# A new loading order for K, V and the later weights, with a new order of all instructions, in a fused long-convolution and feed-forward kernel

## The chip, the cores and the metric

The kernel runs on 1 core of one Trainium2 chip. The metric is the device time of one execution in microseconds; three runs of the kernel before gave 193.63, 193.73 and 193.83.

## The reference

```python
def reference(A_q, A_k, A_v, A_shift_k, A_ssm_k, A_ssm_D, B_x, B_w_gate, B_w_up, B_w_down):
    def _A_ref(q, k, v, shift_k, ssm_k, ssm_D):
        ...                                  # k_shift: k shifted by 0..3 tokens, times 4 taps, summed
        kv = k_shift * v
        ...                                  # y: causal convolution of kv with ssm_k over 2048 tokens (FFT)
        y = y + kv * ssm_D[None, None, :]
        return q * y

    def _B_ref(x, w_gate, w_up, w_down):
        g = jnp.einsum("bsd,df->bsf", x, w_gate)
        u = jnp.einsum("bsd,df->bsf", x, w_up)
        h = _gelu(g) * u
        return jnp.einsum("bsf,fd->bsd", h, w_down)

    x = A_q
    xn = _layernorm(x, axis=-1)
    s = _A_ref(xn, A_k, A_v, A_shift_k, A_ssm_k, A_ssm_D)
    g = _silu(_B_ref(xn, B_w_gate, B_w_up, B_w_down))
    return x + s * g
```

All arrays are bfloat16; q, k and v are 1 x 2048 x 512, the filter ssm_k is 512 x 2048, the gate and up weights 512 x 1792, the down weight 1792 x 512.

## The kernel before

The 2048 tokens stand as 16 tiles of 128, in four quarters (q = 0 to 3) of four tiles.

**Feed-forward.** Each quarter of x is normalized (statistics on VectorE at L832 and L833, a power on GpSimd at L841, the scaled product XN at L850 on ScalarE or L851 on VectorE) and transposed into xnT. Quarters 0 and 1 are transposed on TensorE (L872, four transposes a tile, tasks psxn) and copied out by ScalarE or VectorE; quarters 2 and 3 by a transposing DMA. For quarters 1 to 3 ScalarE's XN needs a bias that GpSimd makes in two steps (NB, L845 and L846). Then 14 units a quarter: a gate product (psg) and an up product (psu), each four matmuls of 512 columns (L626), GELU on ScalarE (GE, L1175) and the product of both on VectorE (HT, L1178). Units 0 and 1 of quarter 0 are made in two halves of 256 columns (L1166, L1168). The down products (psd) follow in pieces of 4, 5 and 5 matmuls, then tanh on ScalarE (L1202) and G on VectorE (L1204).

**Convolution.** It is a two-step transform of 2 x 2048 points. The filter h is transposed on TensorE (L896, psh, two groups of four for each of four pieces), copied to HTr, gets ssm_D added (fold, L910), and goes through step 1 (L938, ps1H0 to ps1H7) and two copies by ScalarE with a sum by VectorE (AH, L947) into DRAM (ZH). K is shifted on VectorE in four pieces: one product with a tap (KAC, L987), three more products (KTM, L991), three sums (KAC, L993) and the product with V's piece (V, L995, in what follows the "V product"). Each step works on 128 x 2048 elements. V's piece then goes through step 1 (L930, ps1K0 to ps1K7, two for each V piece), is copied by ScalarE and stored to DRAM (ZK). Step 2 of both (L1010; psf for the filter, psk for K) reads them back; the spectra are multiplied on VectorE, transformed back (psi, then psy at L1248), and joined with the feed-forward part.

**Banks.** PSUM's eight banks serve all of it. Feed-forward products take one bank each (at most four at once), a step of the transforms takes four, in two pairs of neighbours.

**Order.** All of it is written down as 780 tasks. `SEQ` is a written list of the task numbers; a number with "b" runs on the second engine that the task allows (VectorE in place of ScalarE for a copy out of PSUM, ScalarE in place of VectorE for a normalization). `Sched.run` goes through the list and gives every engine its own tasks in that order, and every buffer its place: it takes the one that is free first by its own plan. `ORDER` is the order in which the loads are numbered, `LAND` the time in ns at which the plan takes each load to have landed. All loads go through SyncE's queue in the order of `SEQ`, so do the stores of K's step 1 (ZK), the loads of step 2 and the three transposing DMAs that make matrices of the inverse transforms (L1021; each waits for the one before it). The stores of the filter's step 1 (ZH) and of the spectra go through ScalarE's queue. Engines wait for each other by semaphores alone, so a task whose input is late holds up all that stands behind it on its engine.

Of the kernel before, what the change touches and what calls it, by code (L numbers as in the profile page):

```python
# [22 lines left out]
LN_EPS = 1e-5  # L23
TURN = 8192
N_WARM = 18
ORDER = "x00 h0 x01 w0 D0 h1 w1 x1 h2 h3 s0 k0 w2 k1 k2 w3 d0 d1 k3 v2 v3 v0 v1 x2 x3"
SEQ = (
# [22 lines left out]
)  # L50
NF_BANKS = 4
ISSUE = 470.0
LAND = {"h2": 15700, "h3": 17000, "sk": 19100, "kh1": 20400, "kh113": 20600, "kz": 10800, "k0": 21900, "wg2": 23400, "wu2": 25100, "k1": 26400, "k2": 27700, "wg3": 29100, "wu3": 30600, "wd0": 32700, "wd1": 34900, "k3": 36100, "v2": 37400, "v3": 38700, "v0": 39900, "v1": 41200, "x0_0": 4400, "h0": 5900, "x0_1": 7000, "D": 4000, "wg0": 7950, "wu0": 8800, "h1": 10100, "wg1": 11600, "wu1": 13100, "x1": 14400}
W_XT, W_SW, W_BK, W_BH, W_ZI, W_BI, W_ZK, W_MI, W_G1 = 765000, 735000, 667000, 688000, 274000, 714000, 690000, 329000, 150000
NC_PAIRS = 4
SMALL = 1.15 * 262144
# [347 lines left out]
def build_kernel(nc, A_q, A_k, A_v, A_shift_k, A_ssm_k, A_ssm_D, B_w_gate, B_w_up, B_w_down, out):  # L404
    with ExitStack() as es0:
# [102 lines left out]
        def dsem(name):  # L508
            return DSem(nc.alloc_semaphore(name), name)
# [88 lines left out]
        def dma(eng, out_ap, in_ap, sem, r, w):  # L598
            trk.dma(eng, lambda e: e.dma_start(out=out_ap, in_=in_ap), sem, r=r, w=w)  # L599
# [3 lines left out]
        def load(name, out_ap, in_ap, w_res, w_buf, nbytes, ring="SP", r=(), rb=()):  # L603
            sem = dsem("d_" + name)
            last_load[0] = S.add([("loads", ISSUE)], lambda e: dma(ring, out_ap, in_ap, sem, r, w_res), r=rb, w=w_buf, nbytes=nbytes, land=float(LAND[name]))

# [212 lines left out]

        for what in ORDER.split():  # L820
            if what[0] == "x" and len(what) == 3:
# [513 lines left out]
```

## Time and profile before

| What | us |
|---|---|
| median of three runs (lowest, highest) | 193.73 (193.63, 193.83) |
| the profiled execution's own time | 193.45 |
| its span, from the first to the last instruction | 191.7 |
| TensorE busy | 185.6 (97%) |
| VectorE busy | 170.0 (89%) |
| ScalarE busy | 135.9 (71%) |
| GpSimd busy | 14.6 (8%) |
| read from HBM, written to it | 27.39 MB, 14.68 MB |

The profile is of one execution. A row of a timeline gives the start and the duration in us, the engine (PE is TensorE, PEld its weight loads, DVE VectorE, ACT ScalarE, POOL GpSimd, SP SyncE), the line, the operation, output and inputs, how many instructions are merged, and in brackets how long the engine stood idle before them and what ended that. A row of waits gives the total in us, the number of times and the longest. Matmuls are pipelined: the next starts before the last one's recorded end. The granted clock of TensorE is at full speed in the whole span.

### The profile page before, as it was taken

To read this page: it belongs to the slowest core of one execution; us is meant where nothing else is said; L and a number is where in the kernel's file an instruction comes from. 1 tells how busy PE (TensorE), PEld (TensorE's weight loads), DVE (VectorE), ACT (ScalarE), POOL (GpSimd) and SP (SyncE) were. 2 spreads that over 40 slices of the span, in tenths; PEclk is the share of its full clock that TensorE was granted. 3 is DMA by queue.
4 is the path that set the end of the run, shared out by engine and by line. 5 is a ranking of instruction groups with operands and counts; after the bars stand their busy time and mean duration, and the time that the engine had idled before them with its cause. 6 is when DMAs were issued, how large, how long until landed. Compare 5 with 4: busy or idle time off the path is not lost.

```text
span 191.7 us, 3540 instructions
## 1 busy us (share of the span) xinstructions
PE 185.6 (97%) x1392; PEld 79.3 (41%) x1392; DVE 170.0 (89%) x248; ACT 135.9 (71%) x184; POOL 14.6 (8%) x31
## 2 busy tenths in 40 slices
PE   7999999999989999999999999999999999999993
PEld 2676443434333333334343434334434444443442
DVE  6889999995999999999698999999999967389865
ACT  3399997978757678889598978778689553244841
POOL 5310560000000000021200000000000000000000
PEclk9999999999999999999999999999999999999999
DMA  5999999999567498358999898995203064966173
GB/s 180 325 384 337 350 370 373 405 345 350 192 209 218 165 297 298 150 199 301 321 253 266 301 364 295 300 349 213 113 0 113 0 219 156 362 251 211 41 299 109
DMA packets 36422, 47.84 MB, mean 250 GB/s; under 512 B 7347, under 2 KB 26039, under 8 KB 36406
## 3 DMA queue, kind: packets, MB, share of 16 engines
q1 hardware_dynamic: 29878, 39.23, 62.4%
q10 hardware_dynamic: 6528, 8.39, 12.5%
q8 instruction: 11, 0.18, 0.4%
q14 instruction: 5, 0.04, 0.1%
HBM read 27.39 MB, written 14.68 MB: 220 GB/s over the span
## 4 chain that ended last, share of the span: by engine, by line
PE 60%; DVE 14%; SPq 13%; DMA 8%; issue 2%; ACT 1%; POOL 0%
PE psall L626 52%; SPq L599 13%; DMA V<-in_A_v_dram 6%; PE psall L1010 5%; DVE KTM L991 3%; DVE KAC L993 2%; PE psall L1248 2%; DMA X<-in_A_q_dram 2%; DVE V L995 2%; DVE stats L832 1%; DVE HT L1178 1%; DVE KAC L987 1%; PE psall L930 1%; DVE G L1204 1%; ACT AST L617 1%
## 5 line engine op out<-in xcount | busy, mean ns | idle before, releaser
L626 PE MATMUL psall<-xnT,Wu 128*128 128x512 bf16 (+1 forms) x232 | 55.1, 373 | 0.7 <-DVE G L1204 0.7
L626 PE MATMUL psall<-xnT,Wg 128*128 128x512 bf16 (+1 forms) x232 | 55.2, 372 | 0.3 <-ACT X L617 0.2
L626 PE MATMUL psall<-Wd,HT 128*128 128x512 bf16 (+2 forms) x238 | 53.1, 367 | 0.0
L1175 ACT ACTIVATE GE<-psall 128x512 bf16<-128x512 f32 x54 | 31.5, 600 | 17.0 <-PE psall L626 11.3
L1178 DVE TENSOR_TENSOR HT<-psall,GE 128x512 bf16<-128x512 f32 x54 | 36.1, 685 | 4.9 <-PE psall L626 4.3
L626 PEld LDWEIGHTS psall<-xnT,Wg 128*128 128x128 bf16 x232 | 21.3, 98 | 28.1 <-issue 1.9
L626 PEld LDWEIGHTS psall<-xnT,Wu 128*128 128x128 bf16 x232 | 21.1, 98 | 28.1 <-issue 3.0
L626 PEld LDWEIGHTS psall<-Wd,HT 128*128 128x128 bf16 x238 | 21.7, 98 | 26.6 <-issue 4.0
L617 ACT ACTIVATE BO<-psall 128x1024 bf16<-128x1024 f32 x18 | 18.0, 1024 | 11.5 <-PE psall L1248 8.3
L1113 DVE TENSOR_TENSOR HSW<-KB,HSW 128x2048 bf16<-128x2048 bf16 x16 | 19.2, 1219 | 0.0
L617 ACT ACTIVATE HSW<-psall 128x1024 bf16<-128x1024 f32 x16 | 15.8, 1032 | 1.5 <-PE psall L1010 1.5
L617 ACT ACTIVATE KB<-psall 128x1024 bf16<-128x1024 f32 x13 | 12.9, 1029 | 3.7 <-PE psall L1010 3.7
L991 DVE TENSOR_TENSOR KTM<-KK,SKB 128x2048 bf16<-128x2048 bf16 x12 | 14.6, 1221 | 0.1
L993 DVE TENSOR_TENSOR KAC<-KAC,KTM 128x2048 bf16<-128x2048 bf16 x12 | 14.7, 1221 | 0.0
L841 POOL TENSOR_TENSOR mv<-mv,NHALF 128x1 f32<-128x1 f32 (+1 forms) x7 | 6.8, 979 | 68.0 <-DVE mv L840 68.0
L832 DVE BATCH_NORM_STATS2 stats<-X 128x6 f32<-128x512 bf16 x16 | 10.5, 679 | 0.4 <-DMA X<-in_A_q_dram 0.4
L617 ACT ACTIVATE AST<-psall 128x1024 bf16<-128x1024 f32 x10 | 10.2, 1023 | 0.9 <-PE psall L930 0.8
L1204 DVE SCALAR_TENSOR_TENSOR G<-G,psall 128x512 bf16<-128x512 bf16 x12 | 7.9, 683 | 2.1 <-ACT G L1202 2.1
L1113 DVE TENSOR_TENSOR KB<-KB,HSW 128x2048 bf16<-128x2048 bf16 x8 | 9.6, 1220 | 0.1
L1136 DVE TENSOR_TENSOR HSW<-HSW 128x2048 bf16<-128x2048 bf16 x8 | 9.5, 1218 | 0.0
L1202 ACT ACTIVATE G<-psall 128x512 bf16<-128x512 f32 x12 | 7.1, 595 | 3.2 <-PE psall L626 3.0
L617 ACT ACTIVATE XN<-psall 128x1024 bf16<-128x1024 f32 x8 | 8.1, 1027 | 1.6 <-PE psall L938 1.4
(84 smaller groups left out, 164.1 us busy)
## 6 DMA issues: line engine op xcount, KB each, us to landing
BH<-ZH SPq DMA_DIRECT2D x8, 512.0 KB, 5.4
HSW<-HSW SPq DMA_DIRECT2D x16, 256.0 KB, 4.2
BK<-ZK SPq DMA_DIRECT2D x8, 512.0 KB, 6.4
ZI<-BO ACTq DMA_DIRECT2D x16, 256.0 KB, 3.2
BI<-ZI SPq DMA_DIRECT2D x8, 512.0 KB, 4.5
ZK<-AST SPq DMA_DIRECT2D x5, 512.0 KB, 3.8
Hn<-in_A_ssm_k_dram SPq DMA_DIRECT2D x4, 512.0 KB, 7.4
KK<-in_A_k_dram SPq DMA_DIRECT2D x4, 512.0 KB, 12.6
```

What stands on the lines that cost most here:

```text
L599: trk.dma(eng, lambda e: e.dma_start(out=out_ap, in_=in_ap), sem, r=r, w=w)
L617: return h.activation(o, i, ACTF.Copy, scale=scale)
L626: return h.matmul(o, lhsT=l, rhs=r, start=st, stop=sp)
L832: t_stats[t] = op([("DVE", 670.0)], lambda e, h, t=t: h.bn_stats(stats[:, t, :], X[:, t, :]), r=[bX[q][t % 4]], w=[bst[t]], rr=[R_X[t]], w ...
L991: op([("DVE", dur)], lambda e, h, j=j, m=m: h.tensor_tensor(KTM[:, m.slot, :, :], kk(j), sk(j), ALU.mult), r=need + [bSKB[j], a], w=[m], r ...
L993: op([("DVE", dur)], lambda e, h, m=m: h.tensor_tensor(KAC[:, a.slot, :, :], KAC[:, a.slot, :, :], KTM[:, m.slot, :, :], ALU.add), r=[m], ...
L1010: trk.op("PE", lambda h: h.matmul(ps(s, i)[b, :], lhsT=wt(col)[a, :], rhs=data(col)[a, :], start=n < 16, stop=n >= len(todo) - 16, tile_po ...
L1113: return hd.tensor_tensor(pair(KB, *(2 * DM * z for z in slots())) if to else x, k, x, ALU.mult)
L1136: return hd.tensor_tensor(x, x, y, ALU.add)
L1175: op([("ACT", act(512))], lambda e, h: h.activation(GE[:, g.slot, :], bank(pg), ACTF.Gelu_apprx_tanh), r=[pg], w=[g], rr=lambda: R_bank(pg ...
L1178: op([("DVE", dve(512, 1))], lambda e, h: h.tensor_tensor(HT[:, q % 2, m, :], bank(pu), GE[:, g.slot, :], ALU.mult), r=[pu, g], w=[bHT[q][m]],
L1204: op([("DVE", dve(512, 1))], lambda e, h, g=g, pc=pc: h.scalar_tensor_tensor(out=g, in0=g, scalar=1.0, in1=pc(), op0=ALU.add, op1=ALU.mult ...
```

## The change

Only the three tables at the head of the kernel change; no instruction is added or taken away. `ORDER` loads the pieces of K and V and the later weights in turn. `LAND` gets new times for the later loads. `SEQ` is a new list in all of its length, found with the plan's transfer times varied over four sets, and 24 tasks, all copies out of PSUM or normalizations, change between ScalarE and VectorE.

```diff
-ORDER = "x00 h0 x01 w0 D0 h1 w1 x1 h2 h3 s0 k0 w2 k1 k2 w3 d0 d1 k3 v2 v3 v0 v1 x2 x3"
+ORDER = "x00 h0 x01 w0 D0 h1 w1 x1 h2 h3 s0 k0 w2 k1 v0 w3 k2 v1 d0 d1 k3 v2 v3 x2 x3"
 SEQ = (
-    "16 17 18 0 19 2 7 8 9 4 20 21 22 23 10 5 3 11 24 67 6 1 68 76 25 26 65 66 73 27 77 78 87 91 74 75 86 90 28 69 70 29 71 30 31 49 48 79 72 32 82 "
...
+    "16 17 18 19 0 20 21 22 23 24 2 25 7 1 26 3 4 27 10 11 8 67 68 76 28 29 30 31 32 6 49 9 12 65 66 73 33 5 34 35 77 78 87 91 74 75 69 70 79 71 72 "
...
 )
-LAND = {... "k0": 21900, "wg2": 23400, "wu2": 25100, "k1": 26400, "k2": 27700, "wg3": 29100, "wu3": 30600, "wd0": 32700, "wd1": 34900, "k3": 36100, "v2": 37400, "v3": 38700, "v0": 39900, "v1": 41200, ...}
+LAND = {... "k0": 22000, "wg2": 24450, "wu2": 26000, "k1": 27350, "v0": 28700, "wg3": 30250, "wu3": 31800, "k2": 33150, "v1": 34500, "wd0": 36750, "wd1": 39000, "k3": 40350, "v2": 41700, "v3": 43050}
```

In `ORDER` x00 and x01 are the halves of quarter 0 of x, h the filter's pieces, w a gate and an up piece (two units each for w0 and w1 and four for w2 and w3), D the skip weights, s the taps, d the halves of the down weight.

Read by engine, with the tasks' names in place of their numbers, these stretches of the list are spoken of below.

TensorE, start, before and after:

```
before: warm-up psxn0_1 psxn0_0 psh0_1 psh0_0 psg0_1(half) psu0_1(half) psg0_0(half) psu0_0(half) psxn0_2 psxn0_3 psh1_1 psh1_0 ...
after:  warm-up psh0_1 psxn0_1 psh0_0 psxn0_0 psg0_0(half) psg0_1(half) psu0_0(half) psxn0_2 psh1_0 psxn0_3 psu0_1(half) psh1_1 psg0_3
        psg0_5 psu0_1(half) psu0_3 psg0_0(half) psu0_5 psh2_0 psg0_1(half) psh3_0 psh2_1 psh3_1 ps1H2 ...
```

VectorE after, from the copy of psh3_0 on (HTr: copies of filter transposes; AH: sums behind filter step 1; kac, ktm: KAC and KTM of K's pieces 0 to 3; KV: the V products):

```
HTr3_0 HT0_1(half) st7 mv1_3 mv1_2 fold HT0_0(half) mv1_0 mv1_1 var1 HTr3_1 AH2 kac0 HT0_4 ktm0 AH3 HT0_2 kac0 AH1 ktm0 HT0_7 kac0 kac1
HT0_8 HT0_9 ktm0 AH7 HT0_10 kac0 HT0_6 ktm1 HT0_13 kac1 AH6 HT0_12 ktm1 HT0_11 AH5 KV0 ... KV1 ... KV2 kac3 HT1_7 ktm3 HT1_1 kac3 HT1_4
ktm3 kac3 KV3 HT1_3 G G ...
```

GpSimd after the taps' load: `SKB3 SKB2 SKB0 power(q1) NB SKB1 NB` (before: four SKB, then power, NB, NB). ScalarE after, in the same stretch: `AH3 AH3 XN4 AH1 AH1 store ZH3 GE0_7 GE0_9 XN6 XN7 store ZH2 GE0_8` (before: `AH3 AH3 GE0_6 AH1 GE0_8 GE0_9 stores XN6 XN5 XN7 GE0_7`).

TensorE around the last V products: before `... psg1_0 psg1_4 psg1_6 ps1K5 psd0_1 psu1_4 psg1_11 ps1K7 psu1_6 psu1_11 ps1K6`, after `... psu1_4 ps1K5 psd0_1 psg1_0 psu1_3 psg1_11 psd0_1 ps1K7 psg1_5 psu1_0 ps1K6 psu1_11 psu1_5 psg1_6`.

SyncE behind the loads: before `G1 MI0 MI1 x3 ZK1 ZK2 ZK0 bh0 ZK3 x2`, after `ZK1 MI0 G1 ZK2 ZK0 x2 x3 ZK3 MI1 bh0` (G1, MI0 and MI1 are the transposing DMAs, bh loads of the filter's step 2).

More of the change, by code (lines that the diff above doesn't have):

```diff
@@ L52 @@
 ISSUE = 470.0
-LAND = {"h2": 15700, "h3": 17000, "sk": 19100, "kh1": 20400, "kh113": 20600, "kz": 10800, "k0": 21900, "wg2": 23400, "wu2": 25100, "k1": 26400, "k2": 27700, "wg3": 29100, "wu3": 30600, "wd0": 32700, "wd1": 34900, "k3": 36100, "v2": 37400, "v3": 38700, "v0": 39900, "v1": 41200, "x0_0": 4400, "h0": 5900, "x0_1": 7000, "D": 4000, "wg0": 7950, "wu0": 8800, "h1": 10100, "wg1": 11600, "wu1": 13100, "x1": 14400}
+LAND = {"x0_0": 4400, "h0": 5900, "x0_1": 7000, "D": 4000, "wg0": 7950, "wu0": 8800, "h1": 10100, "wg1": 11600, "wu1": 13100, "x1": 14400, "h2": 15700, "h3": 17000, "sk": 19100, "kh1": 20400, "kh113": 20600, "kz": 10800, "k0": 22000, "wg2": 24450, "wu2": 26000, "k1": 27350, "v0": 28700, "wg3": 30250, "wu3": 31800, "k2": 33150, "v1": 34500, "wd0": 36750, "wd1": 39000, "k3": 40350, "v2": 41700, "v3": 43050}
 W_XT, W_SW, W_BK, W_BH, W_ZI, W_BI, W_ZK, W_MI, W_G1 = 765000, 735000, 667000, 688000, 274000, 714000, 690000, 329000, 150000
```

42 rows, old and new, of the table SEQ are left out of this document.

## The prediction

> **What bounds the kernel now.** I read the page first, then the chain of waits, then the waits of TensorE and VectorE, then the timelines of the first 30 us and of 70 to 80 us.
>
> ```profile
> span 191.7 us, 3540 instructions
> PE 185.6 (97%) x1392; PEld 79.3 (41%) x1392; DVE 170.0 (89%) x248; ACT 135.9 (71%) x184; POOL 14.6 (8%) x31
> ```
>
> TensorE is busy for 185.6 of 191.7 us. A new order of the same instructions can only give back time in which TensorE stands still, or add some. The waits of TensorE are these (us in total, times, longest):
>
> ```profile
> PE psall L626 <- DVE AST L680: 1.2, 1, 1.2
> PE psall L626 <- DVE G L1204: 0.7, 1, 0.7
> PE psall L930 <- DVE V L995: 0.4, 1, 0.4
> PE psall L930 <- ACT G L1202: 0.3, 1, 0.3
> PE psall L626 <- ACT X L617: 0.2, 1, 0.2
> ```
>
> The first is the start. The other four make 1.6 us; they fall in the stage where K is shifted on VectorE and its transform (L930) runs between the feed-forward products. The chain of waits says what that stage hangs on:
>
> ```profile
> 35.01 12.22 DMA V<-in_A_v_dram
> ...
> 68.30 0.63 PE psall L930 x4
> 68.93 4.65 PE psall L626 x21
> ...
> 156.31 11.11 PE psall L626 x51
> ```
>
> VectorE waits for V's first piece to land, then works without a pause until TensorE's L930 steps have waited for it; after that the chain is nearly all TensorE's. A matmul of 512 columns is 11.11 / 51 = 0.218, a group of four 0.87. The wait itself is in the waits of VectorE:
>
> ```profile
> DVE V L995 <- DMA V<-in_A_v_dram: 2.3, 1, 2.3
> ```
>
> So the price of V's late landing is known: 2.3 us of VectorE, which reached TensorE as at most 1.6 us. The ceiling of the change is about that.
>
> **The change part by part.** *The loads.* V's first piece moves from behind both halves of W_down and K's last piece to right behind K's second; three K and V pieces and W_down come later. The third weight pieces have as many bytes ahead of them as before, so they land when they did. W_down has two pieces of 512 KB more ahead.
>
> ```profile
> L599 SPq DMA_DIRECT2D Wd<-in_B_w_down_dram x2: 3585/3741/3897, 20.9 to 24.8; - x2
> ...
> DMA to landing us min/median/max: 15.4/16.0/16.5
> ...
> 38.30 1.03 PE L626 MATMUL psall<-Wd,HT 128*128 128x512 bf16 x4
> ```
>
> W_down's halves (896 KB each) were issued at 20.9 and 24.8 and landed at 20.9 + 16.5 = 37.4 and 24.8 + 15.4 = 40.2: 2.8 us for a half, so 3.2 for the 1 MB that is now ahead, and the first half lands at 40.6. Its first use was at 38.3 and moves too: in the new list two more up groups (0.87 each), two more transform steps of the filter (0.6, as at 68.30) and two groups of token transposes (0.22, below) stand ahead of it, 3.4 us, which gives 41.7. It costs nothing; were that cover gone, up to 2.3. V's first piece, landed by 47.2, now has 3.4 MB less ahead of it; at the same rate it lands 10 us earlier, by 37. VectorE's new list comes to V's first product ten K steps of 1.13 and fourteen steps of 0.60 (rows below), 19.7 us, behind the first KTM product, which started at 23.59 before and starts later now: after 43 in any case. The 2.3 us wait goes. What is late next has to be looked for on VectorE.
>
> *The front of TensorE.* The new list puts one group of four filter transposes (L896) ahead of each group of four token transposes (L872); before, both token groups came first.
>
> ```profile
> 7.36 0.74 PE L872 MATMUL psall<-ident,XN 128*128 128x128 bf16 x8
> 7.94 1.09 PE L896 MATMUL psall<-ident,Hn 128*128 128x128 f32 x8
> 8.93 0.61 PE L626 MATMUL psall<-xnT,Wg 128*128 128x256 bf16 x4
> 7.79 1.09 ACT L617 ACTIVATE xnT<-psall 128x512 bf16<-128x512 bf16 x2 [5.36 <-PE psall L872]
> ```
>
> Eight token transposes fit between 7.36 and 7.94 with a short wait among them: 0.22 to 0.29 a group of four; a filter group is 0.45 (twelve in 1.47, below). Now: 7.36 + 0.45 + 0.22 + 0.45 = 8.48 is the start of the second token group. ScalarE's copy starts 0.43 after its group (7.36 to 7.79) and takes up to 0.6 (two in 1.09): 9.5. The gate product follows 0.05 later (8.88 to 8.93): 9.55 in place of 8.93. TensorE loses 0.6 here. The table for the DFT (ScalarE, Sin and a table load) moves into the 5.36 us in which ScalarE waited, which is free.
>
> *VectorE up to K's shift.* The copy of the last filter transposes moves to VectorE, and its list reaches it before any K work. TensorE's list from 9.55 to that group (psh3_0) holds seven half groups of 0.44, four groups of 0.87, two token groups and three filter groups: 8.35 us, 18.0 with a little for the changes between them. From a filter group to its copy it is 0.63:
>
> ```profile
> 16.41 1.47 PE L896 MATMUL psall<-ident,Hn 128*128 128x128 f32 x12
> 17.04 1.94 ACT L617 ACTIVATE HTr<-psall 128x1024 bf16<-128x1024 bf16 x2 [0.30 <-PE psall L896]
> ...
> 19.01 1.22 DVE L910 TENSOR_TENSOR HTr<-HTr,Drow 1x512 bf16<-1x512 bf16 x1
> ...
> 21.86 1.22 DVE L987 TENSOR_TENSOR KAC<-KK,SKB 128x2048 bf16<-128x2048 bf16 x1
> 22.99 0.69 DVE L947 TENSOR_TENSOR XN<-XN 128x1024 bf16<-128x1024 bf16 x1
> 23.59 1.22 DVE L991 TENSOR_TENSOR KTM<-KK,SKB 128x2048 bf16<-128x2048 bf16 x1
> ...
> 29.22 0.69 DVE L1178 TENSOR_TENSOR HT<-psall,GE 128x512 bf16<-128x512 f32 x1 [0.27 <-PE psall L626]
> ```
>
> So VectorE starts that copy at 18.6. Start to start a step takes 0.09 less than its duration (21.86 to 22.99 for 1.22). Until the first KTM product the new list has: two copies, the AH sum and one HT product at 0.60, two half HT products at about half of that, one statistic at 0.6, fold and KAC at 1.13, and six small ones of 0.1 with the gaps between dependent ones, 0.8: 6.7. The first KTM starts at 25.3, against 23.59: 1.7 us later. Most of the 2.3 won on V is given back here.
>
> *GpSimd, behind it ScalarE, behind it VectorE.* The new list puts a copy of the taps (SKB) between the two NB steps of the second quarter, and on ScalarE the normalization that needs NB stands ahead of both copies of filter step 1 and of the next three GELUs.
>
> ```profile
> 19.00 2.88 POOL L968 COPY SKB<-SKR 128x512 bf16<-128x512 bf16 x4 [8.60 <-DMA SKR<-in_A_shift_k_dram]
> 25.57 1.92 POOL L841 TENSOR_TENSOR mv<-mv,NHALF 128x4 f32<-128x4 f32 x1 [3.68 <-DVE mv L840]
> 27.57 0.84 POOL L845 TENSOR_TENSOR NB__68<-mv 128x4 f32<-128x4 f32 x1
> 28.50 0.55 POOL L846 TENSOR_SCALAR NB__68<-NB__68 128x4 f32<-128x4 f32 x1
> 29.96 0.81 ACT L850 ACTIVATE XN<-X,NB__68,mv 128x512 bf16<-128x512 bf16 x1 [1.35 <-DVE HT L1178]
> ...
> 90.89 1.03 POOL L841 TENSOR_TENSOR mv<-mv,NHALF 128x4 f32<-128x4 f32 x1 [4.04 <-DVE mv L840]
> ```
>
> VectorE hands over at 22.4, 3.8 into the list above. With the rows of 25.57 and 2.88 / 4 = 0.72 for the copy: 1.92 + 0.84 + 0.72 + 0.55 and 0.3 of gaps, 26.7; the normalization 0.8, two copies at 0.97 (1.94 for two at 17.04): 29.5. VectorE wants their sum at 25.3 + 1.13 + 0.60 + 0.60 + 1.13 = 28.8: a wait of 0.7. With the 1.03 of 90.89 in place of the 1.92 alone, the copies are done at 28.6 and nothing waits. I take 0.6: the row of 25.57 ran beside the same K products, that of 90.89 beside an idle VectorE. The Trainium skill ("SBUF — State Buffer", Who interferes with whom) says that a VectorE instruction with two SBUF inputs and a GpSimd one that reads SBUF exclude each other for a whole instruction; by that the long rows hold, the trace agrees with 1.92 against 1.03, and the sum would be 0.1 higher.
>
> *The K chain.* From the first KTM to the end of the last V product:
>
> ```profile
> 74.65 1.22 DVE L993 TENSOR_TENSOR KAC<-KAC,KTM 128x2048 bf16<-128x2048 bf16 x1
> 75.91 1.22 DVE L995 TENSOR_TENSOR V<-KAC,V 128x2048 bf16<-128x2048 bf16 x1
> ...
> 77.28 0.61 PE L930 MATMUL psall<-V,F 64*128 64x512 bf16 x4 [0.26 <-ACT G L1202]
> ```
>
> Before: 23.59 to 77.13 is 53.5, of it 2.3 of waiting for V and 0.3 at 29.22, which leaves 51.0 of work. The new list holds as much work in this stretch. Where a step needs the one just before it, start to start is 1.26 (74.65 to 75.91) and not 1.13; such pairs fall from four to two, minus 0.2. So 25.3 + 51.0 - 0.2 + 0.6 = 76.7, against 77.13.
>
> *What TensorE does with it.* Its step ps1K7 (the row at 77.28) started 0.15 behind that product: 76.85 now, minus 0.43. By its own list TensorE would be there earlier (1.6 us of waits less, 0.6 of front more, one group less), so VectorE sets it. Of all that stood ahead of ps1K7, one gate group, psg1_6, now comes behind it: 0.87 us that used to fill the time before and is now still to do. After ps1K7 TensorE has no wait in the trace, and none to give back. Sum: -0.43 + 0.87 = +0.44. The end of both lists is the same 128-column group and its store: 0.
>
> *SyncE.* K's first store (ZK1) now comes ahead of the three transposing DMAs, which queue behind its wait for VectorE and ScalarE; x2 and x3 and all other ZK stores stand behind them. What the transposes make is read first by the inverse transform (psi0_0), which comes behind all of K's transform, K's stores and the loads of the first spectra; a later start by some us costs nothing, and were that cover gone, the queue's shift would come on top.
>
> The profiled execution took 193.45 us, 0.3 under the median of 193.73; its rows give a difference, which I add to the median: 194.2.
>
> **The rivals.** *Faster: the wait on V is the whole story.* If the GpSimd chain is short and VectorE's copies wait less than I have it, the last V product ends near 75.5 and TensorE's own list sets ps1K7: then the 1.6 us of waits go and 0.6 of front comes, -0.4 to -1.0, at best 192.7. For it: the 2.3 us row, and that VectorE is 89% busy. The Trainium skill ("Perfetto Trace Analysis", Optimization Strategies) would have it so: when TensorE stands idle for another engine, free the engine that blocks it; by that the time would be the 192.7 of this rival. Against it: TensorE's list has waits of its own in front. Point of decision: the last V product must end before 75.9. Chance 0.2.
>
> *No change.* The gate group that moved and the earlier V product cancel if that product ends near 76.3, within 0.39 us of before, which is 0.2%, about what a measurement here can tell. Chance 0.15.
>
> *Slower by more: a PSUM bank.* ps1K7 needs four banks in two pairs, and three of the eight are freed only by the three VectorE steps behind the last V product. If one of these lies in each free pair, ps1K7 waits one HT product more, 0.6; with the full 0.8 on GpSimd and VectorE waiting for late up groups (0.3) the end is +1.0 to +1.7, up to 195.4. Against it: before, ps1K7 started 0.15 after that product, with three banks just as open. Chance 0.2.
>
> **How the numbers follow.** The forecast, +0.1 to +0.9, gets 0.45, of which 0.1 is under the 0.39. Faster 0.2; same 0.1 + 0.15 = 0.25; slower 0.35 + 0.2 = 0.55. The range goes from -0.8 to +1.5, close to the ends of both rivals, and leaves out about one in twenty at each; another tenth is for waits that no row shows. Cases of both signs are in it; the forecast's own range is 193.8 to 194.6.
>
> **What would show it.** Right: no VectorE wait for V; first gate product near 9.55; first KTM product near 25.3; GpSimd's NB done after 26 and a ScalarE wait for it; the last V product near 76.7 and ps1K7 right behind, waiting for VectorE; no wait of TensorE after 80. Wrong: the first KTM product before 24, or TensorE waiting for W_down near 42, or waits in the second half, which I put at none.

## The result, and the profile after

| What | before | after |
|---|---|---|
| median of 20 runs each, us | 193.75 | 194.29 |
| ratio, with its 95% interval | 1 | 1.0053 (1.0027 to 1.0078) |
| profiled execution, its span, us | 193.45, 191.7 | 193.85, 192.1 |

The change makes the kernel slower by 0.3 to 0.5 per cent; the forecast was 194.2 (192.9 to 195.2), slower. The ratio compares the means of the fast runs, without the four runs of the kernel before that took more than 194.3 us; over all forty runs the means differ by 0.34% and the medians by 0.28% (0.54 us). The number came out, and that is luck: of the steps that lead to it one was 1.1 us too pessimistic, another left out 1.06 us, and the two cancel. The rows of the profile after show both. First the page and the waits of TensorE (us in total, times, longest):

```profile
span 192.1 us, 3523 instructions
PE 184.7 (96%) x1380; PEld 79.5 (41%) x1392; DVE 166.6 (87%) x246; ACT 137.7 (72%) x186; POOL 13.5 (7%) x31
```

```profile
PE psall L626 <- DVE AST L680: 1.2, 1, 1.2
PE psall L626 <- ACT xnT L617: 0.7, 1, 0.7
PE psall L1010 <- DVE BO L620: 0.7, 1, 0.7
PE psall L626 <- issue: 0.5, 3, 0.2
PE psall L626 <- DVE HT L1178: 0.2, 1, 0.2
```

None of the four inner waits of before is left. A new one stands at the start (xnT), and one that the prediction does not have (L1010 behind BO). The 0.5 under "issue" is most likely no wait: this trace has 1380 matmul records for 1392 weight loads, and a missing record would read as a gap of 0.2. VectorE's list has no wait for V; its wait for a store (ZI) is new:

```profile
DVE BO L620 <- DMA ZI<-BO: 1.3, 1, 1.3
```

The timeline shows where the steps came to lie (start, duration, engine, line, operation, idle time before):

```profile
9.55 1.05 PE L626 MATMUL psall<-xnT,Wg 128*128 128x256 bf16 x8 [0.69 <-ACT xnT L617]
...
18.55 0.69 DVE L620 COPY HTr<-psall 128x1024 bf16<-128x1024 bf16 x1 [0.19 <-PE psall L896]
...
25.07 1.22 DVE L991 TENSOR_TENSOR KTM<-KK,SKB 128x2048 bf16<-128x2048 bf16 x1
...
28.55 0.69 DVE L947 TENSOR_TENSOR X<-X 128x1024 bf16<-128x1024 bf16 x1
...
74.35 1.23 DVE L995 TENSOR_TENSOR V<-KAC,V 128x2048 bf16<-128x2048 bf16 x1
...
75.74 0.61 PE L930 MATMUL psall<-V,F 64*128 64x512 bf16 x4
```

The first gate product starts at 9.55 (forecast 9.55), VectorE's copy of psh3_0 at 18.55 (18.6), the first KTM product at 25.07 (25.3). The AH1 sum at 28.55 has no idle time before it (a wait of 0.6 was taken), and the last V product ends at 75.58 (76.7). ps1K7, the 75.74 row, starts 0.16 behind it, against 77.28 before. So TensorE comes out of K's stage early. By psk0, K's first step 2, the moved gate group has been paid back (TensorE has as much work ahead of psk0 in both lists): psk0 starts 0.68 us ahead of before, which is the 1.54 at ps1K7 less 0.87. Before, then after:

```profile
92.50 0.43 PE L1010 MATMUL psall<-BK,TF 32*32 32x512 bf16 x16
```

```profile
91.82 0.43 PE L1010 MATMUL psall<-BK,TF 32*32 32x512 bf16 x16
```

The chain of waits shows where the lead is lost:

```profile
122.43 5.40 DMA ZI<-BO
...
127.92 1.24 DVE BO L620
...
129.20 0.41 PE psall L1010 x8
```

ScalarE copies the first step of an inverse transform (psi1) into buffers BO and issues the store ZI2 at 122.43. It lands 5.40 us later. VectorE's copy of the next one (psi5) was given that buffer and starts only at 127.92; the filter step psf3 on TensorE needs the PSUM bank that this copy frees, so it is cut in two:

```profile
128.12 0.41 PE L1010 MATMUL psall<-BH,TF 32*32 32x512 bf16 x8
129.20 0.41 PE L1010 MATMUL psall<-BH,TF 32*32 32x512 bf16 x8 [0.67 <-DVE BO L620]
129.54 0.82 PE L626 MATMUL psall<-xnT,Wu 128*128 128x512 bf16 x3
```

From the start of psf3 to the next product it is 1.42; an uncut step takes 0.36 (below), so 1.06 is lost. With 0.68 won that gives +0.38; the spans differ by 0.4. The two executions can be laid side by side because TensorE begins its first transposes at nearly the same time in both (7.36 and 7.32); the experiments show that this isn't always so. The lead is that of this pair: counted from the first transposes, psk0 starts at 85.14, 86.15 and 83.78 in three profiles of the kernel before, and at 84.51 and 84.66 in two of the changed one, so against the third it is behind.

### The profile page after: what moved, and what is told of

Its sections match the earlier page's. It is cut to its first block, busy times and chain, and to the rows that moved or that the text cites. A ratio compares the mean times of both kernels' runs of the same rounds, so it can differ in the third digit from the quotient of the medians.

```text
span 192.1 us, 3523 instructions
## 1 busy us (share of the span) xinstructions
PE 184.7 (96%) x1380; PEld 79.5 (41%) x1392; DVE 166.6 (87%) x246; ACT 137.7 (72%) x186; POOL 13.5 (7%) x31
## 4 chain that ended last, share of the span: by engine, by line
PE 77%; DVE 13%; DMA 3%; ACT 2%; issue 2%; POOL 1%; DVEq 0%
PE psall L626 66%; PE psall L1010 5%; DVE KTM L991 3%; DVE HT L1178 3%; DMA ZI<-BO 3%; DVE KAC L993 2%; PE psall L1248 2%; PE psall L930 2%; PE psall L896 1%; ACT BO L617 1%; DVE BO L620 1%; DVE KAC L987 1%; DVE XN L947 1%; POOL NB__68 L845 1%; PE psall L872 1%
## 5 line engine op out<-in xcount | busy, mean ns | idle before, releaser
L626 PE MATMUL psall<-xnT,Wu 128*128 128x512 bf16 (+1 forms) x232 | 56.0, 372 | 0.0
L626 PE MATMUL psall<-Wd,HT 128*128 128x512 bf16 (+2 forms) x226 | 50.6, 366 | 1.1 <-issue 0.5
L617 ACT ACTIVATE BO<-psall 128x1024 bf16<-128x1024 f32 x20 | 20.0, 1026 | 12.3 <-PE psall L1010 6.5
L617 ACT ACTIVATE HSW<-psall 128x1024 bf16<-128x1024 f32 x15 | 14.8, 1024 | 3.7 <-PE psall L1010 3.7
L617 ACT ACTIVATE KB<-psall 128x1024 bf16<-128x1024 f32 x15 | 14.8, 1034 | 1.9 <-PE psall L1010 1.9
L841 POOL TENSOR_TENSOR mv<-mv,NHALF 128x1 f32<-128x1 f32 (+1 forms) x7 | 5.6, 802 | 67.4 <-DVE mv L840 67.4
L617 ACT ACTIVATE X<-psall 128x1024 bf16<-128x1024 f32 x8 | 8.2, 1024 | 1.2 <-DMA ZH<-X 1.2
```

What stands on the lines that cost most here:

```text
L617: return h.activation(o, i, ACTF.Copy, scale=scale)
L626: return h.matmul(o, lhsT=l, rhs=r, start=st, stop=sp)
```

## The experiments

All ratios are against the kernel before on the same chip. In a kernel whose written tables have another number of lines, the profile's line numbers are shifted: by 4 down in the first runs of the V, loads and store edits, by 29 up in the run of the start's edit. Times in two traces are compared from the first transposing matmul on, since the 18 warm-up products ahead of it end at another time in each execution. In the store's run and the second run of the changed kernel:

```profile
1.21 6.87 PE L622 MATMUL psall<-AST 128*128 128x512 bf16 x18 [1.21 <-DVE AST L676]
7.91 0.60 PE L892 MATMUL psall<-ident,Hn 128*128 128x128 f32 x4
```

```profile
1.21 5.37 PE L626 MATMUL psall<-AST 128*128 128x512 bf16 x18 [1.21 <-DVE AST L680]
6.41 0.60 PE L896 MATMUL psall<-ident,Hn 128*128 128x128 f32 x4
```

That is 1.5 us, as much as the edits are worth.

What lies behind psk0 hardly varies. From its start to the end of the last product it is 95.94 or 95.95 us in all eleven profiles, old list or new, in which ZI0 is not stored late, and 96.99, 97.41 and 97.91 in the three in which it is: the changed kernel twice and the start's edit. All other differences between these executions arise ahead of psk0.

**The store.** BO has four places. In the changed list the store ZI0 of psi0 stands behind psi2, so its buffer is held from 102 to 141, and the plan gives psi5's copy the place of ZI2.

```diff
 ScalarE:  ... ZI1
+ZI0
 ... ZI9 ZI8 ZI2 ZI3 ZI11
-ZI0
 ZI4 ...
```

> The changed kernel with one store moved: the store ZI0 of the first inverse transform step goes right behind ZI1 on ScalarE's queue (near 111) in place of 138, so that its buffer is free for the copies of psi5. Theory A (TensorE's wait near 129, 1.05 us over its usual pace, comes from that buffer and is what turned the change from a gain into a loss): the VectorE copy at 126.4 no longer waits for a store, psf3 is not split, the time falls 1.0 us below the changed kernel's, ratio to the kernel before 0.997 to 0.999. Theory B (the wait belongs to one slow store of one execution, or something behind it waits in its place): ratio stays at 1.003 to 1.006.

Median 192.75 (12 runs), ratio 0.9970 (0.9943 to 0.9997).

```profile
126.78 1.21 DVE L616 CAST BO<-psall 128x1024 bf16<-128x1024 f32 x1
...
128.38 0.43 PE L1006 MATMUL psall<-BH,TF 32*32 32x512 bf16 x16
...
128.74 1.04 PE L622 MATMUL psall<-xnT,Wu 128*128 128x512 bf16 x4
```

VectorE's copy starts 0.05 after ScalarE's and psf3 is in one piece. The plan now gives psi0's places to psi1 and psi4's to psi5. ZI2 is issued at 122.69 and lands at 129.32, even later than in the changed kernel (127.83), and in the kernel before it took as long (122.07 to 128.36); in neither of these two does anything wait for it. So it was the place that cost, and not a slower store. Theory A holds: this interval lies below those of the changed kernel, and with the late store the new list loses what it gains. The gain over the kernel before, 0.3%, is at the edge of what its interval can tell.

**The changed kernel again.**

> The changed kernel as it is, on the chip of the others. Theory A (the copy of psi5 waits for the store ZI2 in all executions): ratio 1.003 to 1.007, wait of TensorE near 129 of 0.7 to 1.6 us, store ZI2 over 5 us from issue to landing. Theory B (only in some): no such wait in this profile, and times down to those of the store's edit.

Median 194.13, ratio 1.0051 (1.0023 to 1.0080).

```profile
PE psall L1010 <- DVE BO L620: 1.1, 1, 1.1
```

The wait is there again, larger than in the first profile. It is not one slow store.

**The start.**

```diff
 TensorE: warm-up
-psh0_1 psxn0_1 psh0_0 psxn0_0
+psxn0_1 psxn0_0 psh0_1 psh0_0
 psg0_0(half) ...
```

> The changed kernel with the start of the kernel before on TensorE: both token transposes of the first two tiles ahead of both groups of filter transposes; every PSUM bank as in the changed kernel. First gate product near 8.9 in place of 9.55. Theory A (VectorE, without a pause from 18.55 to 75.57, sets the stage of K, and its chain starts at a copy that waited only 0.19 for TensorE): of the 0.65 us no more than 0.2 to 0.3 reach the end, TensorE waits the rest in front of ps1K7 or at a bank freed by VectorE; ratio 1.002 to 1.004. Theory B (the 0.65 us pass through to the end): ratio 1.000 to 1.002.

Median 193.78, ratio 1.0028 (0.9995 to 1.0060), an interval with both theories in it. In the trace the first gate product comes 1.57 after the first transposing matmul (2.24 in both runs of the changed kernel): the 0.67 are there. psk0 comes 84.12 after it, against 84.51 and 84.66, so 0.4 to 0.5 of them pass through K's stage, more than theory A allows and less than B says. Then they are lost at the store:

```profile
121.62 0.37 ACTq L628 DMA_DIRECT2D ZI<-BO  x1
```

```profile
128.02 1.22 DVE L649 CAST BO<-psall 128x1024 bf16<-128x1024 f32 x1 [2.22 <-DMA ZI<-BO]
```

The store is issued 0.8 us earlier than in the changed kernel's first profile (0.4 of that from a warm-up that ended earlier), and VectorE's copy behind it starts at 128.02 against 127.92: what came early waited longer.

**Both edits.**

> The changed kernel with both edits: the store ZI0 right behind ZI1, and the token transposes of the start ahead of the filter transposes; PSUM banks as with the store's edit alone. With the start's edit alone TensorE ran 0.8 us ahead up to 126 and lost all of it at the copy that waited for the store ZI2 (which landed at 127.9 in both). Theory A (the 0.8 us pass through the stage of K and were lost at that store alone): 0.6 to 0.8 us below the store's edit alone, 191.9 to 192.2, ratio to the kernel before 0.992 to 0.995. Theory B (another late transfer takes them behind the store): as with the store's edit alone, ratio 0.996 to 0.998.

Median 192.32 (191.61 to 192.81), ratio 0.9953 (0.9926 to 0.9980). TensorE's list of waits holds the start (1.2) and one bank:

```profile
PE psall L626 <- DVE HT L1178: 0.2, 1, 0.2
```

From the first transposing matmul to the last product it takes 179.62, the store's edit alone 180.10: the 0.48 that pass K's stage now reach the end. The 0.8 of the expectation had 0.4 of warm-up in it. The interval ends below 1 and below those of the changed kernel: this version beats both. The ratio lies between those of the two theories: what passes is the 0.48, and not the 0.6 to 0.8 of theory A. Against the store's edit alone (0.9970, on another chip) it is 0.2% lower, which the intervals do not tell apart.

**V's load, in the new list.**

```diff
 both edits, loads:
-... w2 k1 v0 w3 k2 v1 d0 d1 k3 v2 v3 x2 x3
+... w2 k1 w3 k2 v1 d0 d1 k3 v2 v3 v0 x2 x3
```

> The kernel with both edits, and V's first piece loaded last of K and V again, as it was before the change; the other loads move up by one. It should land near 47 where VectorE wants it at 44.4. Theory A (V's early landing is what the changed order of loads gives, and VectorE's lateness reaches TensorE as soon as it has no slack left): VectorE waits 2.5 to 3 us, the last V product ends near 78, TensorE waits about as much in front of the transform steps; 2.2 to 2.8 us above both edits, ratio to the kernel before 1.006 to 1.010. Theory B (TensorE has feed-forward groups enough to cover it): under 1 us, ratio 0.996 to 1.000.

Median 195.30 (6 runs), ratio 1.0114 (1.0070 to 1.0159): 1.6% over both edits, more than expected.

```profile
DVE V L995 <- DMA V<-in_A_v_dram: 2.9, 1, 2.9
```

```profile
PE psall L930 <- DVE V L995: 1.8, 2, 1.4
...
PE psall L626 <- ACT GE L1175: 0.6, 1, 0.6
```

V lands at 47.33, VectorE loses 2.9, and TensorE loses it too. In the new list the early V is worth some 3 us (195.30 against 192.32).

**V's load, in the old list.**

```diff
 kernel before, loads:
-... k2 w3 d0 d1 k3 v2 v3 v0 v1 x2 x3
+... k2 w3 d0 d1 v0 k3 v2 v3 v1 x2 x3
```

> The kernel before with one load moved: V's first piece right behind the second half of W_down (ahead of K's last piece, V's third and fourth), all else as before. It should land near 42, and VectorE wants it at 44.9. Theory A (the late V is the whole of the 1.6 us that TensorE waits between 49 and 78): VectorE's wait of 2.3 goes, all four waits of TensorE go, about -1.6 us, ratio to the kernel before 0.992. Theory B (those waits hang on other work too, the G and X copies on ScalarE and VectorE, and VectorE's gain is given back): only the 0.4 and 0.3 in front of the transform of V's pieces go, -0.5 us or less, ratio 0.997 to 1.000.

> The kernel before with V's first piece right behind W_down, once more. Its first run gave 0.9993 (0.9948 to 1.0038), though its profile had none of the waits between 49 and 78. Theory A (the wait is 2.3 to 2.5 us in most executions of the kernel before and costs TensorE 1.6): ratio 0.991 to 0.995 this time. Theory B (part of the wait in some executions only, and other waits, for the third weight pieces and for the first spectra of K, take what is won): 0.996 to 1.000.

Ratios 0.9993 (0.9948 to 1.0038) and 0.9999 (0.9962 to 1.0035): nothing to be seen. V lands at 41.5 and 40.5, and the waits behind it are gone from the profiles, but others stand in them. In the first:

```profile
PE psall L622 <- DMA Wg<-in_B_w_gate_dram: 0.4, 1, 0.4
PE psall L622 <- ACT GE L1171: 0.3, 1, 0.3
PE psall L1006 <- DMA BK<-ZK: 0.3, 1, 0.3
```

In the second:

```profile
PE psall L626 <- ACT X L617: 0.7, 1, 0.7
```

Theory B fits the ratios. From the first transposing matmul to the last product the two take 180.46 and 179.61, the three profiles of the kernel before 181.08, 182.09 and 179.73. The means differ by 0.9 us; a gain of that size (ratio 0.995) is just inside the first interval and just outside the second. Whether some of it is real stays open: both profiled executions (192.52 and 192.34) lie under their medians (193.05 and 192.93), so what the usual run of this kernel waits for is not shown.

**All loads, in the old list.**

```diff
 kernel before, loads:
-... w2 k1 k2 w3 d0 d1 k3 v2 v3 v0 v1 x2 x3
+... w2 k1 v0 w3 k2 v1 d0 d1 k3 v2 v3 x2 x3
```

> The kernel before with the whole new order of loads and the old order of everything else. Theory A (each part of the change has its own price): W_down's first half lands near 40.4 against a first use at 38.3, so TensorE waits about 2 us there; the four later waits (1.6) go with V's early landing; together +0.3 to +0.7 us, ratio 1.002 to 1.004. Theory B (the new order of loads is what the gain comes from, and the old list has room for it): no wait at W_down, -1.6 us, ratio 0.992.

> The kernel before with the new order of loads alone, once more: its profiled execution (191.9) was the fastest of its twelve (median 193.2). Theory A (its usual run has the wait at W_down, about 2 us in place of the 1.2 seen): TensorE waits 1.5 to 2.5 us at the first W_down product, nothing in the stage of K. Theory B (other transfers make the difference): the wait at W_down is near 1.2 again, and in a slower execution TensorE stands still at loads or stores in the second half.

Ratio 1.0003 (0.9967 to 1.0040), neither theory's. TensorE stands still ahead of the first W_down product in both profiles, for 1.2 and 1.1 us and not 2. In the first, W_down had landed 0.35 earlier (38.82) and the list names a copy of ScalarE; in the second it reads:

```profile
PE psall L626 <- DMA Wd<-in_B_w_down_dram: 1.1, 1, 1.1
```

Nothing waits in K's stage in either. The two executions are 1.2 us apart (191.9 and 193.1), and all of it is the warm-up: TensorE's first transposes start at 6.65 and 7.89, and from there to the last product it is 180.24 and 180.22. Neither theory had that.

**The kernel before again, twice.**

> The kernel before once more, for a second profile: its times lie from 191.4 to 194.6 here, and the load of V alone moved forward did not change their median. Theory A (the wait for V and the waits of TensorE behind it belong to all executions): V's first piece lands at 46 or later again, VectorE waits 1.5 to 2.5 us for it, TensorE 1.2 to 1.8 us between 49 and 78. Theory B (they differ from execution to execution, as does V's landing): VectorE waits under 1 us, and TensorE stands still elsewhere, at loads or stores.

> As the run ahead of it, for a third profile of the kernel before: by theory A the same waits again, by theory B others, and a different sum of them in line with the span.

193.63 and 192.13. VectorE's wait for V is 2.5 in the first and 0.5 in the second:

```profile
DVE V L995 <- DMA V<-in_A_v_dram: 2.5, 1, 2.5
```

```profile
45.91 1.23 DVE L995 TENSOR_TENSOR V<-KAC,V 128x2048 bf16<-128x2048 bf16 x1 [0.46 <-DMA V<-in_A_v_dram]
```

In the second TensorE's waits between 49 and 78 are down to one of 0.3. The first run is theory A's, the second theory B's: V's landing at the end of the row of loads moves by 1.3 us from one execution to the next (47.23, 46.78, 45.89), VectorE comes to it at 44.9, 44.3 and 45.4, and the wait is what lies between. That this makes the spread of the kernel before (191.4 to 196.0 in its 20 runs) is not shown: both edits spread over 1.2 us, but the old list with V early spreads over 3.2 and 3.4 us too.

**A gate group back ahead of ps1K7.**

```diff
 both edits, TensorE: ... psg1_11 psd0_1
+psg1_5
 ps1K7
-psg1_5
 psu1_0 ps1K6 ...
```

> The kernel with both edits, and one gate group (psg1_5) moved from behind ps1K7 to ahead of it, as in the kernel before one more group stood ahead of it. Theory A (by the prediction's sum a group ahead of ps1K7 fills time in which TensorE waits for VectorE's last V product, 0.87 us at most): TensorE's wait there was 0.15, so ps1K7 starts 0.6 to 0.75 later, psu1_0 behind it 0.15 to 0.3 earlier, the end 0.1 to 0.2 earlier, which one time can't tell. Theory B (the group takes a bank that another product needs): a new wait of 0.3 us or more behind it.

One run, 192.79. The next step, ps1K6, starts 3.76 behind the start of the last V product with and without the move, and behind it a bank is late, which ScalarE's copies (AST) have to free:

```profile
78.66 1.68 PE L626 MATMUL psall<-xnT,Wu 128*128 128x512 bf16 x7 [0.48 <-ACT AST L617]
```

Theory B, as far as one run shows: from the first transposing matmul to the last product it takes 180.40, against 179.62 with both edits. The place that the change gave to its gate group is the better one.

## Why the prediction was right in its number, and not in all its steps

**Held.** V's landing ended VectorE's wait, W_down's later halves delayed nothing (the first landed at 40.15 and was used from 42.93), the front of TensorE cost 0.68 where 0.62 was worked out (that 9.55 came out to the hundredth owes to a warm-up that ended 0.04 earlier), VectorE's chain began where the list was worked out to begin, and VectorE set ps1K7 with TensorE waiting 0.15 for it. Adding a list up from rows of other instructions worked to 0.2 us over 15 us. V's landing was worked out too late, 37 against 28.45: the prediction counts 3.4 MB less ahead of V, but with K's third piece and the third weights it is 5.0 MB. Nothing hung on it.

**Failed: "1.92 + 0.84 + 0.72 + 0.55", the GpSimd chain.** It was done at 25.24, not 26.7:

```profile
22.16 1.02 POOL L841 TENSOR_TENSOR mv<-mv,NHALF 128x4 f32<-128x4 f32 x1 [0.27 <-DVE mv L840]
23.26 1.20 POOL L845 TENSOR_TENSOR NB__68<-mv 128x4 f32<-128x4 f32 x1
24.40 0.64 POOL L968 COPY SKB<-SKR 128x512 bf16<-128x512 bf16 x1
25.01 0.23 POOL L846 TENSOR_SCALAR NB__68<-NB__68 128x4 f32<-128x4 f32 x1
```

The chain began 0.3 earlier than worked out. The power took 1.02, the shorter of the two rows shown (1.03 and 1.92); it fell beside a copy and a sum and not, like the row of 25.57, beside a K step that had begun ahead of it. That this is the reason is read from the rows and was not tried. The first NB step took 1.20 in place of 0.84, the second 0.23 in place of 0.55. With the chain done early the wait of 0.6 is gone. The rest of the 1.1 us is the start, 0.23 earlier, and a chain that ran 0.3 faster than 51.0 - 0.2. So the step "25.3 + 51.0 - 0.2 + 0.6 = 76.7" was mis-sized by 1.1, and the rival's point of decision, 75.9, was passed: its 0.4 to 1.0 us were won up to psk0 (0.68), though VectorE and not TensorE's own list set ps1K7.

**Failed: "After ps1K7 TensorE has no wait in the trace, and none to give back".** The waits of before were taken for the waits of a new list. The prediction followed the new order through K's stage and not through the inverse transforms, where it also puts ZI0's store 33 us later and gives both copies of psi1 to ScalarE. The prediction named waits in the second half as a sign that it was wrong, and there is one that costs 1.06 (0.67 of it as a wait in the list). It stood in no rival. The store's edit shows the cause.

**The price of V.** The ceiling of 1.6 us came from one execution. That wait differs from execution to execution, in the old list its removal brings no gain that the times show, and in the new list V's late landing costs 3.0.

So +0.44 was a sum of -0.43 and +0.87; measured were -1.54 and +0.87, which make the -0.68, and +1.06, which the sum does not have. The forecast came out because the two errors have opposite signs and nearly the same size.

## What to carry to other kernels

When a whole order is replaced, the new list must be followed to its end: buffers in few places are bound to stores by the order, and a store that is listed late holds its place though its data has long been ready. An early gain can end at the next transfer that does not come earlier: look for the wait that grew by as much as was won. And the price of a wait on a transfer is not known from one profile: here it was 2.3, 2.5 and 0.5 us in three executions of the same kernel.

## What the runs showed of the hardware

The warm-up matmuls start 0.43 apart at first and 0.22 apart later. The change of pace came after 6 to 13 of the 18, so the first transposes behind them began from 6.4 to 7.9 us in 14 profiles, while the profile gives the granted clock as 1.00 in this stretch. In the two profiles of all loads in the old list that is the whole difference; how much of the spread over all runs it makes was not measured. The Trainium skill ("TensorE: Matmul & The Clock Gate", What's actually happening) puts such a change of pace down to a window of activity that runs freely, so that the same kernel counts 6, 11 or 14 slow matmuls; these traces agree.

In two places VectorE and GpSimd seem to hold each other up for a whole instruction. In the profile after, the first NB step on GpSimd (23.26 to 24.46) ends 0.06 after the KAC product beside it, and the first KTM product starts 0.03 after the copy SKB ends (25.04), though the instruction ahead of it began 0.75 before and the usual distance is 0.60. That product reads another piece of the taps (SKB2), copied before 21.9, so it had no need of this copy:

```profile
23.18 1.22 DVE L987 TENSOR_TENSOR KAC<-KK,SKB 128x2048 bf16<-128x2048 bf16 x1
24.32 0.68 DVE L1178 TENSOR_TENSOR HT<-psall,GE 128x512 bf16<-128x512 f32 x1
25.07 1.22 DVE L991 TENSOR_TENSOR KTM<-KK,SKB 128x2048 bf16<-128x2048 bf16 x1
```

The Trainium skill ("SBUF — State Buffer", Who interferes with whom) says that the port pair the two engines share is an exclusive lock, that a VectorE instruction with two SBUF inputs contends for it with a GpSimd instruction that reads SBUF, and that the order of issue decides who blocks. These rows agree. Others do not: the AH sum on VectorE, with both inputs in SBUF, ran from 22.59 to 23.27 beside the power (22.16 to 23.18), and neither took longer than elsewhere (0.68; 1.02 against 1.03 beside an idle VectorE); the second NB step overlaps the KTM product by 0.17. When one holds up the other is not settled here. The prediction drew on the same rule and took it only as a longer duration on GpSimd, where it depends on what happens to run beside it.

The stores ZI of 256 KB that are issued between 110 and 140 in the profile after land 2.1 to 5.4 us later:

```profile
DMA to landing us min/median/max: 2.1/3.0/5.4
```

The slowest is ZI2, issued on ScalarE's queue while loads from SyncE's queue were under way, two of 512 KB of K's spectra (the second landed at 127.37) and two of 256 KB among them. The Trainium skill ("DMA: Bandwidth & Descriptors", Issuing engines are not separate DMA queues) says that transfers of all issuing engines run on the same 16 DMA engines and interleave. That the wait behind ZI2 ended at 127.92 or 128.02 whether it was issued at 122.43 or 121.62 agrees with it; that it was these loads was not tried.
